# A staging buffer shared out anew at the start of a two-layer transformer kernel

## The chip, the cores and the metric

The kernel runs on one core of a Trainium2 chip. The metric is the device time of one execution in microseconds. The core's engines are TensorE (PE; its weight loads are PEld), VectorE (DVE), ScalarE (ACT), GpSimd (POOL) and SyncE (SP). Each takes its instructions strictly in the order in which the program gives them. Every transfer of this kernel is issued by SP, on one queue.

## What is computed

Two layers, each an attention block with a sliding window and an MLP with squared ReLU, over 2048 rows of 640 values. Both layers use the same weights.

```python
def _A_ref(x, wqkv, wo):           # B, S, D = 1, 2048, 640; H = 32; Dh = 20; W = 256
    q, k, v = ...                  # x @ wqkv, split into 32 heads of 20
    scores = einsum("bhqd,bhkd->bhqk", q, k) * (Dh ** -0.5)
    mask = (i - j >= 0) & (i - j < W)
    p = softmax(where(mask, scores, -1e9))
    return einsum("bhqk,bhkd->bhqd", p, v) ... @ wo
def _B_ref(x, w1, b1, w2, b2):     # F = 1536
    h = x @ w1 + b1
    r = where(h > 0, h, 0)
    return (r * r) @ w2 + b2
x = x + _A_ref(_layernorm(x), wqkv, wo)
x = x + _B_ref(_layernorm(x), w1, b1, w2, b2)   # and both once more
```

## The kernel before

**Units.** The rows are cut into 8 groups of 256; with two layers this gives 16 units, `u = 0..15`. A unit runs through `stage_qk` (queries, then keys), `stage_v`, the attention over 8 quads of 4 heads (`max_quad`: scores and row maxima; `max_out`: the maxima are transposed and written as rows `mT` into the query tile; `exp_quad`: scores again, transposed, and exponentials; `pv_quad`: products with the values), `load_o` and `stage_o` (the attention's result is divided by its sums and multiplied with `wo`), `stage_y` (layernorm, transposed) and `stage_f` (the MLP). The attention of unit u runs beside the queries, keys and values of unit u + 1 and the MLP of unit u - 1.

**Precision.** Each operand of a dense product is split into a high and a low fp16 part, and `mm3` makes three matmuls of it. So whatever leaves a PSUM bank for a later product leaves twice: ACT writes the high part, DVE the low part.

**Banks.** Dense products accumulate in two PSUM banks (tag `mm`), which `mm_tile` hands out in turn. A new product needs a bank whose last content has been evicted.

**Queries and keys.** In `stage_qk` the evictions (line 411 on ACT, 414 on DVE) write a tile `qd`, of which there is one (`bufs=1`). When a unit's queries are complete in it, `leave` sends them to DRAM with two transfers (lines 445 and 447), and the keys of the same unit can be evicted into the tile only when these have left. Unit 0 is an exception: its keys go to the first 1280 columns of the staging buffer `hraw` (`stg`, 3072 fp32 columns).

**Staging buffer.** The second MLP weights, 12 blocks of 640 columns, land in `hraw` and are split there into fp16 parts (`convert`: line 194 on ACT for the high part, then either line 196 on DVE or lines 198 on ACT and 199 on POOL). `load_w2` uses four places for the first four blocks and two places (`c % 2`) for the rest, because unit 0's divided rows `od` (in `load_o`, written by line 760 on ACT and 763 on DVE) take the other half. `load_o(0)` waits for blocks 2 and 3 to be split. The MLP's hidden tile `hh` takes the place of `hraw` afterwards, so its first write waits for all of `w2`.

**Order.** The order on each engine is set when the kernel is built: `Job`, `post`, `pump` and `need` keep a clock for each engine from costs written in the code and emit an instruction when its planned start comes up; dense products are generators that are advanced between attention steps (`flow` for unit 0, `together` for the others). A change of a dependency or a place therefore moves instructions on all engines nearby.

**The end.** For the last unit, `together` leaves part of the dense work of unit 14 unissued. `load_o(15, True)` follows, `upto(dense, 10e3)` issues 10 us (by the planner's costs) of that work while the load runs, then `stage_o(15)`, then the remainder, then the last MLP.

Of the kernel before, what the change touches and what calls it, by code (L numbers as in the profile page):

```python
# [11 lines left out]
F16 = mybir.dt.float16  # L12
# [4 lines left out]
P = 128  # L17
S = 2048
D = 640
# [4 lines left out]
T = 256  # L24
NG = S // T
NU = NL * NG
KC = D // P
# [17 lines left out]
def kernel(ctx: ExitStack, tc: tile.TileContext, x, wqkv, wo, w1, b1, w2, b2, out):  # L45
# [4 lines left out]
    sb = ctx.enter_context(tc.tile_pool(name="sb", bufs=1))  # L50
# [78 lines left out]
    def dma(fn, size, *deps, n=1, cost=450.0, prio=1, **kw):  # L129

        return post("S", n * cost, fn, *deps, prio=prio, size=size, **kw)
# [29 lines left out]
    banks2 = []  # L161
# [25 lines left out]
    w1raw = w1_s.rearrange("p a k n -> p (a k n)").bitcast(F32)  # L187
    w2raw = w2_s.rearrange("p a k n -> p (a k n)").bitcast(F32)
    hraw = sb.tile([P, 2 * FC * T // 2], F32, name="stg", tag="hh", bufs=1)
    gate, gate0 = [Job("S", 0.0, None, [], 0.0, 0) for i in range(2)]  # L190

    def convert(st, hi, low, n, load, *deps, prio=2, dve=True):

# [46 lines left out]
    def load_w2():  # L240
        for c in range(FC):
            first = [w1j[f] for f in (c // 4 * 2, c // 4 * 2 + 1, 6 + c // 4 * 2, 7 + c // 4 * 2)]
            slot = c if c < 4 else c % 2
            st = hraw[:, D * slot:D * (slot + 1)]
            load = dma(lambda st=st, c=c: nc.sync.dma_start(st, w2[c * P:(c + 1) * P, :]), P * D * 4,
                       *([w2j[c - 4 if c < 6 else c - 2]] if c > 3 else [gate]), prio=2, idle=True,
                       land=WLAND)
            w2j[c] = convert(st, w2_s[:, 0, c], w2_s[:, 1, c], D, load, *first, dve=c % 3 == 2)

# [135 lines left out]
    def stage_qk(u, which=(0, 1)):  # L385
        need(*pre.pop(u, ()))
        yT = yTs[u]
        qds = {}

        order = [(j, c0) for j in which for c0 in range(0, KC, 2)]  # L390
        if u == 0:
            order.sort(key=lambda t: t[1])
        for j, c0 in order:
            if j not in qds:
                if j == 0:
                    qts[u] = sb.tile([P, NP, T], F16, name="qt", tag="qt", bufs=2)
                if j and u == 0:
                    qd = hraw[:, :KC * T].bitcast(F16).rearrange("p (c a n) -> p c a n", a=2, n=T)
                elif j and u > 2:
                    qd = beside(u)[:, 1].rearrange("p (c a n) -> p c a n", a=2, n=T)  # L400
                else:
                    qd = sb.tile([P, KC, 2, T], F16, name="qd", tag="qd", bufs=1)
                qds[j] = qd
            qd = qds[j]
            dst = kts[u % 3] if j else qts[u]
            n = min(2, KC - c0)
            acc, jobs = mm_tile([P, 2, T], "acc")
            s = QS / (YS * WS)

            def high(qd=qd, acc=acc, c0=c0, n=n):  # L410
                nc.scalar.activation(qd[:, c0:c0 + n, 0, :], acc[:, :n, :], AF.Copy, scale=s)

            def low(qd=qd, acc=acc, c0=c0, n=n):
                nc.vector.scalar_tensor_tensor(qd[:, c0:c0 + n, 1, :], acc[:, :n, :], s, qd[:, c0:c0 + n, 0, :],  # L414
                                               op0=ALU.mult, op1=ALU.subtract)

            def evict(wait, n=n, c0=c0, high=high, low=low, jobs=jobs, j=j, dst=dst, qd=qd):
                lo_ = post("D", 70 + 267 * n, low, post("A", 60 + 212 * n, high, wait=wait, prio=0), prio=0)
                jobs.append(lo_)
                if u == 0:  # L420
                    leave(u, j, dst, qd, lo_, c0, n)
                elif c0 + n == KC:
                    leave(u, j, dst, qd, lo_, 0, KC)

            for c in range(n):
                lo = j * D + (c0 + c) * P
                need(wqj[lo // P])
                yield from mm3(acc[:, c, :], lambda a, k: wq_s[:, a, k, lo:lo + P],
                               lambda b, k: yT[:, b, k, :], KC, 109, evict if c == n - 1 else None)
# [5 lines left out]
    def leave(u, j, dst, qd, ready, c0, n):  # L435

        if c0 == 0:
            rows_of[u, j] = tc.dram_tile([D, 3, T], F16, name=f"qk{u}_{j}")
        dr = rows_of[u, j]
        drv = dr.rearrange("(c p) t n -> p c t n", p=P)  # L440

        p0, p1 = c0 * P // (2 * DH), (c0 + n) * P // (2 * DH)

        def write():
            nc.sync.dma_start(drv[:, c0:c0 + n, j:j + 2, :].rearrange("p c t n -> p c (t n)"),
                              qd[:, c0:c0 + n].rearrange("p c a n -> p c (a n)"))
            nc.sync.dma_start(drv[:, c0:c0 + n, 2 - 2 * j, :], qd[:, c0:c0 + n, 0, :])

        def spread():
            for e in range(2):  # L450
                nc.sync.dma_start(dst[64 * e:64 * e + 3 * DH, p0:p1, :],
                                  dr.rearrange("(p e d) t n -> e (d t) p n", e=2, d=DH)[e][:, p0:p1])

        wrote = dma(write, n * P * 3 * T * 2, ready, n=2, prio=0)

        def load(*deps):
            job = dma(spread, int((p1 - p0) * 2 * DH * 3 * T * 2 * (1.7 if u > 2 else 1.1)), wrote, *deps, n=2, prio=0)
            for p in range(p0, p1, 2):
                trips[u, j, p // 2] = job
            if u == 0 and j == 1 and p1 == NP:  # L460
                job.gates.append(gate)
            if u == 0 and j == 1 and p0 == 0:
                job.gates.append(gate0)

        if u == 2 and 2 not in rowset:
            held.append((j, load))
        else:
            load(*(rowset.get(u, ()) if j else ()))
# [231 lines left out]

    ols = {}

    def load_o(u, late=False, free_=()):

        l, g = divmod(u, NG)
        if late:
            val = sb.tile([P, KC, T], F32, name="ov", tag="qt", bufs=2)
            od = sb.tile([P, KC, 2, T], F16, name="od", tag="yT", bufs=1)
        elif u == 0:
            val = krow[2][:, :KC * T].rearrange("p (c n) -> p c n", n=T)  # L710
            od = hraw[:, 2 * D:4 * D].bitcast(F16).rearrange("p (c a n) -> p c a n", a=2, n=T)
        else:
            raw = sb.tile([P, 2, KC, T], F32, name="od", tag="hh", bufs=1)
            val = raw[:, 0]
            od = raw[:, 1].rearrange("p c n -> p (c n)").bitcast(F16).rearrange("p (c a n) -> p c a n", a=2, n=T)
# [4 lines left out]
            nc.sync.dma_start(rs, ods[u][DH:].to_broadcast([4, H, T]))  # L720
            nc.sync.dma_start(val, ods[u][:DH].rearrange("(c d) h n -> (d h) c n", d=4))

        loaded = dma(load, P * (KC + 1) * T * 4, *wrote, *free_, n=2, prio=0)
        if u == NU - 1:
            both = sb.tile([P, 2, D], F32, name="x1", tag="qt", bufs=2)
            x1 = [both[:, i] for i in range(2)]
# [177 lines left out]
    late = []  # L904
# [20 lines left out]
            yield c  # L925

    def upto(dense, cost):
        while cost > 0:
            c = next(dense, None)
            if c is None:  # L930
                break
            step(c)
            cost -= c
# [87 lines left out]
    for n in range(NQ):  # L1021
        todo += [("s", n)] + ([("r", n + LEAD - GQ)] if n % GQ == 1 else []) + [("m", n + LEAD), ("v", n)]
    flow(todo, rest)
    load_o(0, False, (w2j[2], w2j[3]))
    left_over = 3 * (QKC + VC + LNC) - used[0]
    rate[0] = 320.0
    for u in range(1, NU):
# [52 lines left out]
```

## Time and profile before

| | |
|---|---|
| median of 3 runs | 1647.06 us (1645.21 to 1647.41) |
| the profiled execution | 1641.93 us, of which its span is 1640.2 us |
| mean granted TensorE clock | 0.987 |
| PE busy | 1575.6 us, 96% of the span |
| DVE, ACT, POOL busy | 1030.1, 748.4, 636.6 us |
| PE busy in the stretches 41 to 82, 123 to 164 us | 28.37 and 29.58 of 41 us |
| granted clock there | 0.83 and 0.81 |

The span is what the profile covers; 1.73 us of the profiled execution lie outside it. The median of the other runs stands 5.13 us above the profiled execution. Busy shares are of the span; the granted clock is the share of full speed that TensorE had.

### The profile page before, as it was taken

The page shows a single profiled execution, that of the slowest core. Times are in us where ns is not written, and L with a number is a line of the kernel's source. Part 1 is how long each engine was busy: PE and PEld are TensorE (multiplying, and loading weights), DVE is VectorE, ACT ScalarE, POOL GpSimd, SP SyncE. Part 2 cuts the span into 40 slices and gives each one's busy share as a digit, 9 for nine tenths or more (in the row PEclk, how much of TensorE's full clock was granted, in tenths as well). Part 3 has the DMA queues.
Part 4 walks back from the last instruction along what each step waited for, and adds up shares of the span by engine and source line. Part 5 has one row for each costly group of instructions (what it writes and reads, how often), then busy time and mean ns, then how long its engine had stood idle before and what let it go on. Part 6 is the DMA issues. An engine that isn't in the chain of part 4 may idle for free.

```text
span 1640.2 us, 52819 instructions
## 1 busy us (share of the span) xinstructions
PE 1575.6 (96%) x21670; PEld 1172.6 (71%) x21670; DVE 1030.1 (63%) x3231; ACT 748.4 (46%) x1616; POOL 636.6 (39%) x1309
## 2 busy tenths in 40 slices
PE   7697899999999999999999999999999999999989
PEld 5564677777777777777777777777777777776667
DVE  7567657675665766566565756657665666757341
ACT  4465534535444454544434354444545444453512
POOL 1343533535344353434414343443534344354412
PEclk9898999999999999999999999999999999999999
DMA  8465214343342434345253434425343452431020
GB/s 255 123 183 157 62 63 109 65 118 86 102 102 65 124 75 112 80 108 114 51 137 74 124 85 103 102 69 119 73 112 81 106 117 51 110 71 54 27 65 17
DMA packets 231517, 157.95 MB, mean 96 GB/s; under 512 B 79468, under 2 KB 215020, under 8 KB 231276
## 3 DMA queue, kind: packets, MB, share of 16 engines
q1 hardware_dynamic: 231276, 154.59, 38.4%
q8 instruction: 170, 2.79, 0.7%
q14 instruction: 71, 0.58, 0.1%
HBM read 84.68 MB, written 52.95 MB: 84 GB/s over the span
## 4 chain that ended last, share of the span: by engine, by line
PE 83%; DVE 6%; ACT 4%; DMA 4%; POOL 2%; issue 1%; SPq 1%; DVEq 0%; ACTq 0%; POOLq 0%
PE acc L256 63%; PE pv L674 10%; PE bb L542 5%; PE bb L613 5%; DVE bb L555 3%; ACT pt L625 2%; DMA qk<-qd 1%; DMA xt<-in_B_b_dram 1%; PE tr L567 1%; POOL x L805 1%; DVE mx L555 1%; POOL pt L644 0%; ACT r L843 0%; DMA w_s<-in_B_w_dram 0%; DMA ov<-o 0%
## 5 line engine op out<-in xcount | busy, mean ns | idle before, releaser
L555 DVE CUSTOM_DVE_ANT_0 bb<-bb,maskb 128x384 f32<-128x384 f32 (+2 forms) x1024 | 510.5, 567 | 114.9 <-PE bb L542 106.4
L625 ACT ACTIVATE pt<-bb 128x512 f32<-128x512 f32 (+1 forms) x736 | 376.5, 601 | 233.9 <-PE bb L613 220.5
L640 POOL TENSOR_SCALAR_AFFINE_SELECT pt<-pt 128x256 f32<-128x256 f32 x448 | 194.8, 439 | 529.7 <-ACT pt L625 507.9
L256 PE MATMUL acc<-y,w_s 128*128 128x256 f16 x2880 | 330.8, 273 | 4.8 <-DVE y L304 1.5
L256 PE MATMUL acc<-w_s,hh 128*128 128x320 f16 x2304 | 326.2, 299 | 0.0
L256 PEld LDWEIGHTS <-w_s 128*128 128x128 f16 x2880 | 277.9, 98 | 57.3 <-issue 23.5
L256 PE MATMUL acc<-yT,wq_s 128*128 128x256 f16 x2400 | 281.0, 275 | 14.0 <-DVE qd L414 11.9
L256 PEld LDWEIGHTS <-hh 128*128 128x128 f16 x2304 | 221.7, 98 | 96.8 <-issue 12.5
L256 PEld LDWEIGHTS <-wq_s 128*128 128x128 f16 x2400 | 232.9, 99 | 57.5 <-issue 26.5
L644 POOL TENSOR_SCALAR_AFFINE_SELECT pt<-pt 128x256 f32<-128x256 f32 x512 | 217.3, 446 | 65.7 <-ACT pt L625 64.6
L853 DVE TENSOR_TENSOR hh<-r,hh 128x256 f16<-128x256 f32 x192 | 91.9, 500 | 205.9 <-ACT hh L850 199.3
L674 PE MATMUL pv<-pt,vt 128*32 128x128 f32 (+1 forms) x3840 | 189.6, 332 | 2.0 <-POOL pt L644 1.4
L847 POOL TENSOR_TENSOR r<-r 128x256 f32<-128x256 f32 x192 | 113.5, 612 | 181.2 <-ACT r L843 179.9
L686 ACT COPY ot<-pv 128x256 f32<-128x256 f32 x128 | 47.6, 372 | 277.4 <-PE pv L674 277.4
L555 DVE DVE_READ_ACCUMULATOR2_ANT mx<- 128x1 f32 x1024 | 145.4, 142 | 0.1
L256 PE MATMUL acc<-wq_s,yT 128*128 128x320 f16 x960 | 142.1, 301 | 0.1
L674 PEld LDWEIGHTS pv<-pt,vt 128*32 128x32 f32 x3840 | 104.4, 110 | 45.6 <-POOL pt L644 4.9
L256 PE MATMUL acc<-wo_s,od 128*128 128x320 f16 x900 | 130.5, 299 | 3.9 <-DVE x L785 1.7
L843 ACT ACTIVATE r<-acc,b1s 128x256 f32<-128x256 f32 x192 | 80.6, 471 | 98.0 <-PE acc L256 97.2
L256 PEld LDWEIGHTS <-yT 128*128 128x128 f16 x960 | 93.1, 99 | 40.4 <-issue 6.5
L256 PEld LDWEIGHTS <-od 128*128 128x128 f16 x900 | 85.5, 98 | 44.7 <-issue 8.3
L613 PE MATMUL bb<-qt,kt 62*64 62x128 f16 (+3 forms) x3840 | 100.3, 235 | 9.1 <-DVE mx L555 8.4
(84 smaller groups left out, 1169.5 us busy)
## 6 DMA issues: line engine op xcount, KB each, us to landing
qt<-qk SPq DMA_DIRECT2D x30, 480.0 KB
kt<-qk SPq DMA_DIRECT2D x30, 480.0 KB
qk<-qd SPq DMA_DIRECT2D x17, 640.0 KB
o<-ot SPq DMA_DIRECT2D x256, 42.0 KB
od<-o SPq DMA_DIRECT2D x13, 640.0 KB
qk<-yl SPq DMA_DIRECT2D x13, 640.0 KB
qk<-qd SPq DMA_DIRECT2D x17, 320.0 KB
xt<-in_A_x_dram SPq DMA_DIRECT2D x16, 320.0 KB
```

What stands on the lines that cost most here:

```text
L256: nc.tensor.matmul(acc, lhs(a, c), rhs(b, c), start=(k == 0), stop=(k == 3 * nk - 1))
L542: nc.tensor.matmul(to, qt[r, p, i * P + 64 * h:i * P + 64 * h + 64], kt[r, p, a:b], start=True, stop=True, tile_position=(64 * e, 64 * h))
L555: nc.vector.tensor_tensor_reduce(out=v, in0=v, in1=mask, scale=1.0, scalar=-3.0e38, op0=ALU.add, op1=ALU.max, accum_out=accum)))
L613: nc.tensor.matmul(bb[e][64 * h:64 * h + 64, k, o:o + w], kt[r, p, ko + 64 * h:ko + 64 * h + 64], qt[r, p, q:q + w], start=True, stop=True ...
L625: nc.scalar.activation(box["pt"][:, :o], bb[e][:, k, :o], AF.Exp, scale=SCALE / (QS * QS))
L640: nc.gpsimd.affine_select(out=m, in_=m, pattern=[[0, 2], [-1, P]], compare_op=ALU.is_gt, fill=0.0, base=0, channel_multiplier=1)
L644: nc.gpsimd.affine_select(out=m, in_=m, pattern=[[0, 2], [1, P]], compare_op=ALU.is_ge, fill=0.0, base=0, channel_multiplier=-1)
L674: nc.tensor.matmul(pv[32 * jj:32 * (jj + 1), q0 * P:(q0 + qn) * P], vf[:, c:c + 32], pj[:, j, :], start=(k == 0), stop=(k == len(steps) - ...
L686: nc.scalar.copy(ot[:, qd % 2], pv)
L843: nc.scalar.activation(box["r"], acc[:, f, :], AF.Relu, bias=b1s[:, f0 + f:f0 + f + 1], scale=1.0 / (YS * WS))
L847: nc.gpsimd.tensor_tensor(box["r"], box["r"], box["r"], op=ALU.mult)
L853: nc.vector.tensor_sub(hh[:, 1, f, :], box["r"], hh[:, 0, f, :])
```

## The change

Four edits. Unit 1's keys are evicted into the second 1280 columns of `hraw` instead of the one `qd` tile. Unit 0's divided rows `od` get a tile of their own, under the tag `qd`, and no longer wait for weight blocks. All twelve blocks of the second MLP weights go through four places, and those of the second half wait until unit 1's keys have left. `upto` goes on until each open bank has been given its eviction, so the kept work ends with a whole product.

```diff
-    gate, gate0 = [Job("S", 0.0, None, [], 0.0, 0) for i in range(2)]
+    gate, gate0, gate1 = [Job("S", 0.0, None, [], 0.0, 0) for i in range(3)]
     def load_w2():
-            slot = c if c < 4 else c % 2
+            slot = c % 4
-                       *([w2j[c - 4 if c < 6 else c - 2]] if c > 3 else [gate]), prio=2, idle=True,
+                       *([w2j[c - 4]] if c > 3 else [gate, gate1][:1 + c // 2]), prio=2, idle=True,
     def stage_qk(u, which=(0, 1)):
-                if j and u == 0:
-                    qd = hraw[:, :KC * T].bitcast(F16).rearrange("p (c a n) -> p c a n", a=2, n=T)
+                if j and u < 2:
+                    qd = hraw[:, u * KC * T:][:, :KC * T].bitcast(F16).rearrange("p (c a n) -> p c a n", a=2, n=T)
     def leave(u, j, dst, qd, ready, c0, n):
         wrote = dma(write, n * P * 3 * T * 2, ready, n=2, prio=0)
+        if u == 1 and j:
+            wrote.gates.append(gate1)
-    def load_o(u, late=False, free_=()):
+    def load_o(u, late=False):
         elif u == 0:
             val = krow[2][:, :KC * T].rearrange("p (c n) -> p c n", n=T)
-            od = hraw[:, 2 * D:4 * D].bitcast(F16).rearrange("p (c a n) -> p c a n", a=2, n=T)
+            od = sb.tile([P, KC, 2, T], F16, name="od", tag="qd", bufs=1)
-        loaded = dma(load, P * (KC + 1) * T * 4, *wrote, *free_, n=2, prio=0)
+        loaded = dma(load, P * (KC + 1) * T * 4, *wrote, n=2, prio=0)
     def upto(dense, cost):
-        while cost > 0:
+        while cost > 0 or not all(banks2):
-    load_o(0, False, (w2j[2], w2j[3]))
+    load_o(0)
```

Two lines are added above the attention, so line numbers from 457 on are two higher in the changed kernel (its line 582 is line 580 of before). The text below uses the numbers of before.

The order of PE's instructions is the same in both up to the end of the last unit. Three places where the order or the target of other engines moves:

First, ACT around the eviction of unit 1's first keys. `qd` is the one tile, `stg` the staging buffer, `pt` the exponentials, `ot` the attention's result. Before:

```order
L686 COPY ot<-pv 128x256
L198 ACTIVATE w_s<-w_s 128x640
L194 ACTIVATE wo_s<-w_s 128x640
L411 ACTIVATE qd<-acc 128x2x256
L625 ACTIVATE pt<-bb 128x512 x2
```

and now:

```order
L688 COPY ot<-pv 128x256
L198 ACTIVATE w_s<-w_s 128x640
L194 ACTIVATE wo_s<-w_s 128x640
L411 ACTIVATE stg<-acc 128x2x256
L627 ACTIVATE pt<-bb 128x512 x2
```

The order is the same; the eviction's target is another buffer.

Second, SP after the last part of unit 0's attention result `o` has been sent. `rs` and `kt_79` receive the sums and the undivided rows of `load_o(0)`, `qk_1` takes unit 2's keys, and `stg` the blocks of the second MLP weights. Before:

```order
L691 DMA o_808<-ot 21x2x256 x4
L245 DMA stg<-in_B_w_dram 128x640
L445 DMA qk_1_1829<-qd 128x5x512
L447 DMA qk_1_1829<-qd 128x5x256
L245 DMA stg<-in_B_w_dram 128x640 x2
L720 DMA rs<-o_808 128x1x256
L721 DMA kt_79<-o_808 128x5x256
L580 DMA qt<-mT 1x8x128 x4
L451 DMA qt<-qk_0_1494 60x16x256 x2
```

and now:

```order
L693 DMA o_807<-ot 21x2x256 x4
L245 DMA stg<-in_B_w_dram 128x640
L722 DMA rs<-o_807 128x1x256
L723 DMA kt_79<-o_807 128x5x256
L445 DMA qk_1_1829<-qd 128x5x512
L447 DMA qk_1_1829<-qd 128x5x256
L451 DMA qt<-qk_0_1493 60x16x256 x2
L737 DMA x_1779<-in_A_x_dram 128x640
L737 DMA x_1780<-in_A_x_dram 128x640
L245 DMA stg<-in_B_w_dram 128x640
L582 DMA qt<-mT 1x8x128 x4
```

The two loads of `load_o(0)` have moved ahead of unit 2's keys and of two weight blocks; the row copies `mT` have moved behind a weight block.

Third, DVE at the same stage: `rs` is inverted, `kt_79` multiplied with it, `od` (before: `stg`) takes the low part, `yT` is the transposed layernorm for unit 3. Before:

```order
L196 SCALAR_TENSOR_TENSOR w_s<-stg,w_s 128x640
L572 TENSOR_SCALAR mT<-tr 16x128
L573 SCALAR_TENSOR_TENSOR mT<-tr,mT 16x128
L304 TENSOR_TENSOR yT<-tr,yT 128x3x128
L304 TENSOR_TENSOR yT<-tr,yT 128x2x128
L304 TENSOR_TENSOR yT<-tr,yT 128x3x128
L304 TENSOR_TENSOR yT<-tr,yT 128x2x128
L753 RECIPROCAL rs<-rs 128x64 x2
L756 TENSOR_TENSOR kt_79<-kt_79,rs 128x5x64 x2
L196 SCALAR_TENSOR_TENSOR w_s<-stg,w_s 128x640
L763 TENSOR_TENSOR stg<-kt_79,stg 128x5x64 x2
```

and now:

```order
L196 SCALAR_TENSOR_TENSOR w_s<-stg,w_s 128x640
L755 RECIPROCAL rs<-rs 128x64 x2
L574 TENSOR_SCALAR mT<-tr 16x128
L575 SCALAR_TENSOR_TENSOR mT<-tr,mT 16x128
L758 TENSOR_TENSOR kt_79<-kt_79,rs 128x5x64 x2
L755 RECIPROCAL rs<-rs 128x64
L765 TENSOR_TENSOR od<-kt_79,od 128x5x64 x2
L758 TENSOR_TENSOR kt_79<-kt_79,rs 128x5x64
L304 TENSOR_TENSOR yT<-tr,yT 128x3x128
L304 TENSOR_TENSOR yT<-tr,yT 128x2x128
L755 RECIPROCAL rs<-rs 128x64
```

The division and the first half of `od` stand ahead of the layernorm's transposes now, and the weight block has moved behind. The fourth low part of `od` and three fills of `kt_79`, which before stood after the row maxima of the next quad, stand ahead of them.

At the end, PE issues 108 of the 144 matmuls of unit 14's second MLP product ahead of `stage_o(15)`, where it issued 76 before; a product is 36 matmuls.

## The prediction

> **What bounds the kernel now.** I read the page first, then PE's waits, then the stretches in which those waits lie, engine by engine. In the page, PE is busy 96% of the span, and the chain that ended last is PE for 83% of it.
>
> ```profile
> PE 1575.6 (96%) x21670; PEld 1172.6 (71%) x21670; DVE 1030.1 (63%) x3231; ACT 748.4 (46%) x1616; POOL 636.6 (39%) x1309
> PE 83%; DVE 6%; ACT 4%; DMA 4%; POOL 2%; issue 1%; SPq 1%; DVEq 0%; ACTq 0%; POOLq 0%
> ```
>
> So only 64.6 us are to be had from filling PE's gaps, and whatever time PE spends at a lower clock. PE's waits (total us, times, longest) name where:
>
> ```profile
> PE acc L256 <- DVE qd L414: 11.9, 1, 11.9
> PE bb L613 <- DVE mx L555: 8.4, 11, 3.0
> ...
> PE acc L256 <- ACT stg L760: 4.1, 1, 4.1
> PE tr L300 <- DVE xt L286: 3.1, 1, 3.1
> PE acc L256 <- DVE stg L763: 2.9, 2, 2.1
> ```
>
> The first is a wait for keys to be evicted, the third and fifth are for `od`. The change touches these, and four short ones at the end. It leaves the second and fourth alone: PE's order there is the same, and the work around them hardly moves.
>
> **Unit 1's keys.** Rows in the timeline give start, duration, engine, operation, and in brackets the idle time before.
>
> ```profile
> 45.83 5.63 PE L256 MATMUL acc<-yT,wq_s 128*128 128x256 f16 x50
> 69.62 2.29 PE L256 MATMUL acc<-yT,wq_s 128*128 128x256 f16 x10 [11.89 <-DVE qd L414]
> 77.03 0.52 PE L613 MATMUL bb<-qt,kt 62*64 62x256 f16 x16
> 57.81 0.74 ACT L194 ACTIVATE wo_s<-w_s 128x640 f16<-128x640 f32 x1 [1.78 <-DMA w_s<-in_A_wo_dram]
> 68.24 0.60 ACT L411 ACTIVATE qd<-acc 128x512 f16<-128x512 f32 x1 [9.70 <-DMA qk<-qd]
> 57.83 3.27 SPq L447 DMA_DIRECT2D qk<-qd  x1
> 69.78 2.83 SPq L580 DMA_DIRECT2D qt<-mT  x4
> 57.83 10.31 DMA qk<-qd
> 66.00:68.00 2.00, 0.00 (x0) 0.00 (x0) 0.00 (x0) 0.00 (x0) 0.00 (x0) 0.50 0.21 68
> ```
>
> PE stops at 57.73 (69.62 - 11.89) because its next product needs the bank of the first keys. ACT cannot evict them before unit 1's queries have left `qd`: their write (the row of the chain, 10.31) ends at 68.14. With a place of their own the keys wait for ACT alone, which is held until 58.50 by a weight conversion (57.81 + 0.74, overlapping the next). From ACT's start to PE's restart the trace shows 69.62 - 68.24 = 1.38, so PE would restart at 59.88. The wait falls from 11.89 to 2.15: 9.7 us.
>
> What is late next: PE's `exp_quad` (line 613) follows 77.03 - 69.62 = 7.41 after the restart, at 67.29, and needs the row maxima `mT` in `qt`. SP's four copies of them started 0.16 after PE's restart (69.78), so they are due at 60.0; but SP is issuing the queries' second write until 61.10, so they go out from 61.1 to 63.9 (2.83) behind a write that lands only at 68.14. In the trace the same copies are used 7.25 after their issue without a wait, with nothing ahead of them. So the added wait lies between 0 (they pass) and about 3 (they land after 68.14 by the length of their own issue). The last row (PE to POOL busy, granted clock 0.50, DMA share 0.21) shows a fifth of the DMA engines' time still busy just before 68; I take the middle, 1.5. [...] No row before shows small copies behind a large write with a waiting reader.
>
> Net for this edit 8.2 us. Ends: 5.0 (the rows cost 3 and PE's clock falls once more, 1.7, half of the 3.5 below) and 10.9 (no wait for rows, and the restart at full clock: 10 matmuls took 2.29, where 50 of them took 5.63 at 45.83, so 1.2). Later loads and conversions keep their order behind this place and move up with it; DMA was one fifth used at the end of these ten microseconds, so what covers them stays.
>
> **Unit 0's divided rows.**
>
> ```profile
> 143.39 0.83 PE L300 MATMUL tr<-ident,xt 128*128 128x128 f32 x5 [0.53 <-DVE yT L304]
> 148.34 0.71 PE L256 MATMUL acc<-wo_s,stg 128*128 128x320 f16 x2 [4.12 <-ACT stg L760]
> 149.88 2.85 PE L256 MATMUL acc<-wo_s,stg 128*128 128x320 f16 x10 [0.83 <-DVE stg L763]
> 152.65 1.49 PE L542 MATMUL bb<-kt,qt 60*64 60x128 f16 x36
> 154.08 1.98 PE L674 MATMUL pv<-pt,vt 128*32 128x256 f32 x32
> ...
> 161.15 1.08 PE L256 MATMUL acc<-wo_s,stg 128*128 128x320 f16 x6 [2.10 <-DVE stg L763]
> 162.16 1.50 PE L613 MATMUL bb<-qt,kt 62*64 62x256 f16 x32
> 163.59 4.00 PE L256 MATMUL acc<-wo_s,stg 128*128 128x320 f16 x22
> 261.55 2.21 PE L256 MATMUL acc<-wo_s,od 128*128 128x320 f16 x15
> 126.32 0.36 SPq L245 DMA_DIRECT2D stg<-in_B_w_dram  x1
> 135.53 2.20 SPq L245 DMA_DIRECT2D stg<-in_B_w_dram  x2
> 137.83 0.59 SPq L720 DMA_DIRECT2D rs<-o  x1
> 140.92 2.75 SPq L580 DMA_DIRECT2D qt<-mT  x4
> 145.29 0.95 DVE L753 RECIPROCAL rs<-rs 128x64 f32<-128x64 f32 x2
> 147.45 0.83 ACT L760 CAST stg<-kt 128x320 f16<-128x320 f32 x2
> 134.09 1.42 POOL L199 TENSOR_TENSOR w_s<-stg,w_s 128x640 f16<-128x640 f32 x1 [0.23 <-ACT stg L198]
> ```
>
> (In the times of before; all of it moves up by the 8.2.) The load of `rs` leaves at 137.83, behind two weight blocks that SP held until 135.53 for POOL's conversions. Now it stands ahead of both and of unit 2's keys, behind the block at 126.32; with some 3 us for the last part of `o` to land, that is 8 us earlier. DVE can divide before the layernorm's transposes instead of behind them. `od` wants the one `qd` tile: unit 2's keys go out at about 130, and even with the 10.31 of unit 1's queries they have left it at 140.6, before DVE's first product behind `mT` (140.92). So that adds nothing. But the transposes are now late: two of DVE's divisions (0.95) and two of ACT's casts (0.83) stand ahead of them, so the x5 transposes start near 145.1 instead of 143.39. The first product follows 1.6 later, at 146.75, instead of 148.34, without the second wait (0.83) and the third (2.10).
>
> The clock adds to it. The 22 matmuls at 163.59 take 182 ns each, against 147 for the 15 at 261.55 (4.00/22 and 2.21/15): after 2.10 us of waiting PE runs slow for some 3.5 us. [...]
>
> Stepping through PE's rows from 146.75: 12 matmuls still slow (3.5), scores and values 1.2 and 1.6 (1.49 and 1.98 slow), 26 matmuls 3.8, which is 156.9; 0.3 more for DVE's maxima, which the third wait hid so far; then scores 0.9 (1.50 slow) and 22 x 0.147 = 3.2. The product ends at 161.3 instead of 167.6 (163.59 + 4.00). I take 6.2 us. Ends: 8.5 (the transposes not late, no slow restart) and 3.0 (only the last two waits, 2.93, go).
>
> **Four places for the weights.** Unit 0's hidden tile must wait for all of `w2`, so ACT's casts come late:
>
> ```profile
> 191.13 1.02 ACT L850 CAST hh<-r 128x256 f16<-128x256 f32 x3 [3.46 <-DVE w_s L196]
> 197.05 0.21 PE L542 MATMUL bb<-kt,qt 60*64 60x128 f16 x1 [1.20 <-ACT pt L625]
> ```
>
> With four places the blocks are in sooner, and the casts stand between other work. PE loses only 1.20 here, from exponentials queued behind the casts; I take 0.8, between 0 and 1.5.
>
> **The end.**
>
> ```profile
> 1563.12 10.49 PE L256 MATMUL acc<-w_s,hh 128*128 128x320 f16 x76
> 1574.10 2.34 PE L256 MATMUL acc<-wo_s,od 128*128 128x320 f16 x15 [0.48 <-DVE kt L880]
> ...
> 1582.58 2.20 PE L256 MATMUL acc<-wo_s,od 128*128 128x320 f16 x15 [0.58 <-DVE x L785]
> ...
> 1593.85 0.49 PE L300 MATMUL bb<-ident,xt 128*128 128x128 f32 x3
> 1577.89 0.49 DVE L763 TENSOR_TENSOR od<-ov,od 128x320 f16<-128x320 f32 x1 [0.53 <-ACT od L760]
> 1587.19 0.61 DVE L286 TENSOR_SCALAR xt<-x,bmv 128x640 f32<-128x640 f32 x1 [0.66 <-POOL bmv L284]
> ```
>
> 76 matmuls are two products and four matmuls of a third, which keep one bank open, so the four `wo` products share the other and each waits for an eviction (0.48, and 0.58 three times). With 108 both banks are free. From 1563.12, 204 matmuls of 10.49/76 = 0.138 end at 1591.3 instead of 1593.85: 2.4 us (2.2, the waits alone, to 2.6). The 32 matmuls moved ahead had hidden the last layernorm: it ends (1587.19 + 0.61) 3.0 after the last `wo` product (1582.58 + 2.20), so at 1589.3 behind products that now end at 1586.3. That is still 2.0 ahead of PE. The last part of `od` (1577.89 + 0.49) is needed at 1582.1.
>
> **Sum.** 8.2 + 6.2 + 0.8 + 2.4 = 17.6 us off the profiled execution of 1641.93: 1624.3. That execution ran 5.13 below the median of 1647.06; set against the median the sum gives 1629.5, and I predict 1630. With all terms at their ends the gain is 10.2 to 23.5, so 1624 to 1637.
>
> **Rivals.** *The row copies become the wait* (14%). Unit 1's wait turns into one for `qt` and the first term stays at its low end or less: 14.4 in all, 1633. For it speaks the write still draining at 66 to 68, against it that the copies are only 2 KB each.
>
> *The divided rows are no sooner* (15%). DVE and ACT are given the division ahead of the transposes, and PE waits there instead; the second term falls to about 1: 12.4, 1635. For it speaks that the order now puts this work ahead of what PE waits for at 143.39. With the first rival 1638.
>
> *The gain is given back* (5%). All of the front's work is moved up against loads that do not move, and PE waits at a later weight load for as long as it saved: only the end's 2.4 stays, 1645. Against it speaks that PE's list of waits holds none for a weight load, and that DMA was mostly idle in the wait that goes (0.21 in the row above).
>
> *SP is blocked* (3%, slower). The copies of `mT` (140.92) stand behind a weight block that waits for POOL's conversion of the first block, which ended at 135.51 (134.09 + 1.42). Their reader is the scores at 162.16, near 157 then; less 2.75 for the copies, a conversion ending after 154 costs PE one for one, 18.7 later than it does. The kernel is slower from another 20.9 on (17.6 and the 3.3 below): with a conversion 45 us late it would be 1656. POOL's wait ahead of it was 0.23.
>
> **Chances.** My forecast holds 63%. What a measurement can tell from no change is 0.2%, 3.3 us. Faster takes the forecast and the first two rivals, 0.92; the third rival is within 0.2%, 0.05; slower 0.03. The range runs from 1622, past the best sum, to 1639, past the first two rivals together.
>
> **What would show it.** Right: PE's wait for line 414 near 60 is about 2 us instead of 11.89, no wait of PE for lines 760 or 763 near 135, four `wo` products without gaps at the end. Wrong: a wait of a few us at line 613 near 67, or one for line 304 before the first `wo` product.

## The result, and the profile after

The changed kernel takes 1629.20 us (median of 5 runs, 1623.36 to 1631.56), the kernel before 1645.21 beside it (1641.41 to 1647.41): a ratio of 0.9899, with a 95% interval of 0.9873 to 0.9925. The ratio is estimated from all runs and isn't the quotient of the two medians. By the medians the gain is 16.0 us, by the interval 12.3 to 20.9. The profiled execution took 1627.51, its span 1625.8, at a granted clock of 0.993. A second series, with a second profile, gave 1628.71 (1622.82 to 1631.08) against 1644.63: 0.9896 [0.9879, 0.9914], span 1623.2. Both profiles are used below, since they differ in an instructive way.

The page after, its engines and its chain:

```profile
PE 1573.4 (97%) x21670; PEld 1172.1 (72%) x21670; DVE 1030.1 (63%) x3231; ACT 749.9 (46%) x1616; POOL 641.0 (39%) x1309
PE 87%; DVE 5%; ACT 3%; DMA 2%; issue 1%; POOL 1%; SPq 0%; DVEq 0%; POOLq 0%; ACTq 0%
```

PE does the same work in 2.2 us less busy time; the other 12.2 us between the spans are idle time that went. PE's waits after:

```profile
PE bb L615 <- DVE mx L557: 10.3, 15, 3.0
...
PE tr L300 <- DVE xt L286: 4.4, 1, 4.4
PE bb L615 <- DMA qt<-mT: 3.8, 1, 3.8
...
PE acc L256 <- DVE stg L414: 1.1, 1, 1.1
```

The wait of 11.89 us for the keys' eviction is 1.1, and the three for `od` near 148 to 161 are gone. New is a wait of 3.8 us for the row copies `mT`. Two waits that the prediction left alone have grown: the layernorm's (line 300) from 3.13 to 4.40, and those for the row maxima `mx` from 8.4 to 10.3 in total (9.0 in the second profile).

To see where the time lies, the program is cut into six stretches at seven places. Each place is the start of one matmul that all kernels share: the transposition of the row maxima (`tr<-ident,mx`), and at the last place the last recorded group on PE. Us between these places, from PE's timeline; the starts in the row of before are 57.45, 84.05, 140.30, 180.72, 204.19, 1534.97 and 1617.25:

| kernel | keys | up to the rows | divided rows | places | middle | end |
|---|---|---|---|---|---|---|
| before | 26.60 | 56.25 | 40.42 | 23.47 | 1330.78 | 82.28 |
| after, first profile | 19.96 | 56.74 | 35.83 | 23.08 | 1329.66 | 79.28 |
| after, second profile | 18.60 | 56.00 | 32.78 | 23.08 | 1331.18 | 79.29 |
| keys alone | 20.17 | 55.96 | 40.29 | 23.48 | 1331.96 | 83.87 |
| rows and places alone | 26.15 | 57.34 | 32.81 | 23.08 | 1331.10 | 81.94 |
| rows alone | 27.01 | 57.35 | 35.47 | 28.31 | 1330.40 | 81.85 |
| end alone | 26.39 | 57.33 | 40.03 | 23.48 | 1330.83 | 80.97 |
| after, with two places | 20.29 | 59.28 | 35.68 | 28.40 | 1329.17 | 79.30 |

In the first profile the keys' stretch gives 6.6, the divided rows' 4.6, the places' 0.4 and the end 3.0; in the second 8.0, 7.6, 0.4 and 3.0. Ahead of the first place, where nothing is changed, the profiles of this table differ by up to 2.6 us, and the two profiles of the changed kernel differ by 3.05 in one stretch: a difference of 2 us between two profiles is no evidence by itself. In the rows keys alone and end alone the last stretch holds some 1.6 us of lower clock that the others don't have: the same 179 matmuls take 21.31 and 21.37 there and 19.70 in every other row (see the last section).

### The profile page after: what moved, and what is told of

It is laid out like the page before. It is cut to its first block, busy times and chain, and to the rows that moved or that the text cites. A ratio compares the mean times of both kernels' runs of the same rounds, so it can differ in the third digit from the quotient of the medians.

```text
span 1625.8 us, 52818 instructions
## 1 busy us (share of the span) xinstructions
PE 1573.4 (97%) x21670; PEld 1172.1 (72%) x21670; DVE 1030.1 (63%) x3231; ACT 749.9 (46%) x1616; POOL 641.0 (39%) x1309
## 4 chain that ended last, share of the span: by engine, by line
PE 87%; DVE 5%; ACT 3%; DMA 2%; issue 1%; POOL 1%; SPq 0%; DVEq 0%; POOLq 0%; ACTq 0%
PE acc L256 66%; PE pv L676 10%; PE bb L615 5%; PE bb L544 5%; DVE bb L557 2%; ACT pt L627 1%; PE tr L569 1%; DMA w_s<-in_A_wo_dram 1%; DVE mx L557 0%; DMA qk<-qd 0%; DMA xt<-in_B_b_dram 0%; DMA w_s<-in_A_wqkv_dram 0%; POOL pt L646 0%; DVE mT L574 0%; DMA qt<-mT 0%
## 5 line engine op out<-in xcount | busy, mean ns | idle before, releaser
L256 PE MATMUL acc<-wo_s,od 128*128 128x320 f16 x960 | 140.3, 301 | 2.4 <-DVE od L765 1.7
L256 PEld LDWEIGHTS <-od 128*128 128x128 f16 x960 | 91.9, 98 | 46.2 <-issue 7.4
L615 PE MATMUL bb<-qt,kt 62*64 62x128 f16 (+3 forms) x3840 | 100.8, 235 | 14.6 <-DVE mx L557 10.3
```

Source lines behind the costliest of these rows:

```text
L256: nc.tensor.matmul(acc, lhs(a, c), rhs(b, c), start=(k == 0), stop=(k == 3 * nk - 1))
L615: nc.tensor.matmul(bb[e][64 * h:64 * h + 64, k, o:o + w], kt[r, p, ko + 64 * h:ko + 64 * h + 64], qt[r, p, q:q + w], start=True, stop=True ...
```

## The experiments

**One part of the change at a time.** Kernel before, with the keys' edits only:

```diff
...
-                if j and u == 0:
-                    qd = hraw[:, :KC * T]...
+                if j and u < 2:
+                    qd = hraw[:, u * KC * T:][:, :KC * T]...
-                       *([w2j[c - 4 if c < 6 else c - 2]] if c > 3 else [gate])
+                       *([w2j[c - 4 if c < 6 else c - 2]] if c > 3 else [gate, gate1][:1 + c // 2])
+        if u == 1 and j:
+            wrote.gates.append(gate1)
```

> The kernel before with one part of the change alone: unit 1's keys leave from the staging buffer, and the second-weight blocks that would overwrite that buffer wait for it. Divided rows, the places for the second weights and the kept work at the end stand as before. Theory (the term is what the trace of the changed kernel shows between the transposes at the unit's end, 6.6 us, and it depends on nothing else in the change): 6 to 7 us faster than before, with TensorE's wait for the row copies near 69 us at about 3.8 us and the wait for the bank near 60 us at about 1. Rival (the sum of the prediction): 8.2 us faster, with a row-copy wait near 1.5. Rival (the gain leaned on the other parts and is given back at the next wait, for the divided rows): under 2 us faster, with the wait at the output projection near 142 longer by the missing amount.

Measured: 1638.04 against 1644.63, 0.9950 [0.9934, 0.9966], so 6.6 us faster by the medians. The interval, 5.6 to 10.9 us, holds the theory's 6 to 7 and the first rival's 8.2, so the time doesn't decide between them. In the trace the keys' stretch is 6.4 shorter, in PE's timeline with these rows:

```profile
59.17 2.29 PE L256 MATMUL acc<-yT,wq_s 128*128 128x256 f16 x10 [1.68 <-DVE stg L414]
68.48 0.88 PE L615 MATMUL bb<-qt,kt 62*64 62x256 f16 x16 [1.91 <-DMA qt<-mT]
70.28 3.03 PE L256 MATMUL acc<-wq_s,yT 128*128 128x320 f16 x12
```

The wait for the copies is 1.91, not the expected 3.8, because the products ahead of it ran slower (10 of them 2.29, in the changed kernel 1.25); the scores (68.48) start 11.26 after the first place (57.22), in the changed kernel 11.05 after it. So the end of this wait is fixed by the copies, however early PE arrives. The gain is not given back later: the next stretches are those of before.

The kernel before with the two edits that belong to `od`, rows and places:

```diff
-            slot = c if c < 4 else c % 2
+            slot = c % 4
-                       *([w2j[c - 4 if c < 6 else c - 2]] if c > 3 else [gate])
+                       *([w2j[c - 4]] if c > 3 else [gate])
-            od = hraw[:, 2 * D:4 * D]...
+            od = sb.tile([P, KC, 2, T], F16, name="od", tag="qd", bufs=1)
-    load_o(0, False, (w2j[2], w2j[3]))
+    load_o(0)
```

> The kernel before with two parts alone: the first divided rows have a buffer of their own and the second weights have four places; the keys and the kept work at the end stand as before. Theory (the rows' term is 6.6 us at the output projection, of which about 2 are given back at the layernorm behind it, plus 0.2 for the places): 4 to 5.5 us faster than before, with TensorE's wait for the layernorm's rows at about 4.4 us, before 3.1. Rival (the give-back belongs to the keys, which bring the block forward against loads that did not move): 6 to 7 us faster and a layernorm wait of about 3.1.

Measured: 1638.77, 0.9954 [0.9939, 0.9969], 5.9 us faster by the medians. The interval, 5.1 to 10.0 us, doesn't decide between the theory and the rival; the layernorm's wait does. It is 4.40 without the keys' edits, so the give-back belongs to the rows and places, as expected. In the profile the rows' stretch is 7.6 shorter.

The kernel before with the edit in `upto` only:

```diff
-        while cost > 0:
+        while cost > 0 or not all(banks2):
```

> The kernel before with one part alone: the last unit's kept work ends with a product, so that 108 matmuls stand ahead of the last output projection where there were 76. Theory (the gap ahead of that projection closes): 2.2 to 3.0 us faster than before, all of it behind 1560 us. Rival (part of the 3.0 us between the profiles is chance of one run): 2.0 or less.

Measured: 1642.52 (10 runs), 0.9982 [0.9973, 0.9992], 2.1 us faster by the medians, 1.3 to 4.4 by the interval, so the time doesn't decide between the theory and the rival. The traces do: from the start of the 108 matmuls (76 before) to the first transposition of the last layernorm (line 300) PE takes 27.71 here and in the changed kernel, and 30.28 to 30.73 in the four kernels without this edit. So 2.6 to 3.0 us are gained, and not by chance of one run. By the medians the three parts add up to 6.6 + 5.9 + 2.1 = 14.6, and the whole gives 16.0: within the intervals they add up.

**Rows and places taken apart.** The changed kernel with two places again:

```diff
-            slot = c % 4
+            slot = c if c < 4 else c % 2
-                       *([w2j[c - 4]] if c > 3 else ...
+                       *([w2j[c - 4 if c < 6 else c - 2]] if c > 3 else ...
```

> The changed kernel with two places for the MLP's second weights instead of four; everything else as changed. Theory (four places take away only the waits of 1.2 us and less near 187 us): 0 to 1 us slower than the changed kernel, so about 15 us faster than before, with the layernorm wait at about 4.4 us still. Rival (four places let later blocks be split earlier, beside the layernorm, and so cause its longer wait): the layernorm wait falls to about 3.1 us, and the kernel is as fast as the changed one or up to 1 us faster.

Measured: 1635.21, 0.9929 [0.9912, 0.9945]; 0.9929 against 0.9899 is 4.9 us slower than the changed kernel, whose runs in both series (1622.82 to 1631.56) all lie below the runs here (1631.64 to 1635.38). Its trace has a wait of 3.98 for ACT's ReLU in the stretch called places, and a layernorm's wait of 3.84. Both expectations missed. So the remaining part was tried in the kernel before by itself, the `od` and `load_o(0)` lines of the diff above without the `slot` lines:

> The kernel before with the own place for the first divided rows alone; the second weights keep two places from the fourth block on, and keys and end stand as before. The run with two places in the changed kernel lost 4.9 us between the second and the third transposes of the MLP (173.8 to 202.2, against 170.8 to 193.9), to a wait of 4.0 us for ScalarE's ReLU, which stood behind the blocks' conversions. Theory (the two parts are one: without four places the gain of the rows turns into that wait): about 7 us gained to the output projection, 4 to 5 of them lost again near 190, so 2 to 3 us faster than before, against 5.9 for the two parts together. Rival (that wait comes from the keys, which move the rest forward as well): 5 to 6 us faster, and no wait above 1.5 near 190.

Measured: 1642.66 (10 runs) against 1643.98, 0.9995 [0.9983, 1.0008]: no gain, less even than the theory left, though by its mechanism. By the profile the rows' stretch is 5.0 shorter, and the next one 4.8 longer. PE, then ACT in that stretch of rows alone:

```profile
190.24 2.90 PE L256 MATMUL acc<-y,w_s 128*128 128x256 f16 x25
197.11 3.36 PE L256 MATMUL acc<-y,w_s 128*128 128x256 f16 x15 [3.97 <-ACT r L843]
190.40 3.04 ACT L625 ACTIVATE pt<-bb 128x512 f32<-128x512 f32 x6 [3.80 <-PE bb L613]
193.28 0.78 ACT L194 ACTIVATE w_s<-stg 128x640 f16<-128x640 f32 x1
195.01 1.32 ACT L850 CAST hh<-r 128x256 f16<-128x256 f32 x4 [0.95 <-DVE w_s L196]
196.24 1.56 ACT L843 ACTIVATE r<-acc,b1s 128x256 f32<-128x256 f32 x4
```

PE waits 3.97 for a bank that ACT's ReLU (line 843) must empty. The ReLU stands behind the hidden tile's casts (line 850), and the first of these waits for the last weight block, because `hh` takes the place of `hraw`. How many blocks are late is read from the groups by line, for line 194, one of which belongs to each block. The three rows are: before in the rows' stretch (140.30 to 180.72), rows alone in its rows' stretch, and rows alone in the stretch behind:

```profile
L194 ACT ACTIVATE w_s<-stg 128x640 f16<-128x640 f32 x7 | 5.0, 739 | 0.0
L194 ACT ACTIVATE w_s<-stg 128x640 f16<-128x640 f32 x5 | 3.7, 743 | 0.0
L194 ACT ACTIVATE w_s<-stg 128x640 f16<-128x640 f32 x3 | 2.3, 775 | 0.0
```

Before, PE's waits for `od` gave two more blocks time to pass through the two places, and one was left for the next stretch. Without those waits three are left. With four places all eight are through before it (the changed kernel, 134.95 to 170.78):

```profile
L194 ACT ACTIVATE w_s<-stg 128x640 f16<-128x640 f32 x8 | 5.9, 738 | 0.0
```

So the own tile for `od` brings nothing without the four places. Four places without the own tile were not run; in the kernel before, `od` lies in two of the four.

**What holds the row copies.** In the changed kernel, SP's queue and behind it PE's reader:

```profile
51.27 0.79 SPq L232 DMA_DIRECT2D w_s<-in_B_w_dram  x1
53.16 4.58 SPq L445 DMA_DIRECT2D qk<-qd  x1
57.78 3.49 SPq L447 DMA_DIRECT2D qk<-qd  x1
61.37 4.71 SPq L582 DMA_DIRECT2D qt<-mT  x4
69.30 0.88 PE L615 MATMUL bb<-qt,kt 62*64 62x256 f16 x16 [3.77 <-DMA qt<-mT]
70.72 3.41 PE L256 MATMUL acc<-wq_s,yT 128*128 128x320 f16 x12
```

The copies are issued when the queries' write has been, and used 7.93 after the first issue. Two edits were tried. In the first, the load of line 232 (640 KB) goes out behind the copies:

```diff
...
-            load = dma(lambda st=st, f0=f0: nc.sync.dma_start(...), P * KC * 2 * P * 4, gate,
+            def fetch(st=st, f0=f0): nc.sync.dma_start(...)
+            load = dma((lambda fetch=fetch: held_w1.append(fetch)) if f0 == 0 else fetch, ..., gate,
...
+            if (u, G) == (0, 1):
+                held_w1.pop()()
```

> The changed kernel with one transfer moved: the first load of the MLP's first weights (640 KB) is issued on SP right behind the four row copies near 66 us instead of ahead of unit 1's queries near 51. Question: what makes TensorE wait 3.8 us near 69 for the row copies, which SP issues as the last of some 14 us of issues without a pause (1.0 + 4.6 + 3.5 + 4.7 us). Theory (the issues of the queries' write are slow because the load ahead of them still fills the DMA engines): the two queries' issues fall from 4.6 and 3.5 us to under 2 each, the row copies come 4 to 6 us sooner, the wait near 69 is under 0.5, and the kernel is 2 to 4 us faster than the changed one, so 18 to 20 faster than before. Rival A (SP's issues of these four transfers cost what they cost, for the number of pieces they are cut into): only the load's own 0.8 to 1.2 us leaves the row, the wait falls to 2.5 to 3, and the kernel gains about 1. Rival B (the later load is missed where it is used): a new wait of some us for the first block of it, and no gain.

Measured: 1625.83 (1624.51 to 1626.44), 0.9886 [0.9864, 0.9908]. SP and PE of this kernel, and a stretch of 1 us with its DMA share:

```profile
53.76 0.38 SPq L448 DMA_DIRECT2D qk<-qd  x1
54.19 3.60 SPq L450 DMA_DIRECT2D qk<-qd  x1
60.08 3.65 SPq L585 DMA_DIRECT2D qt<-mT  x4
63.79 0.43 SPq L235 DMA_DIRECT2D w_s<-in_B_w_dram  x1
67.36 0.92 PE L620 MATMUL bb<-qt,kt 62*64 62x256 f16 x16 [1.57 <-DMA qt<-mT]
62.00:63.00 1.00, 1.00 (x18) 0.73 (x11) 1.00 (x9) 0.53 (x2) 0.69 (x1) 1.00 0.27 104
```

The queries' first issue falls from 4.58 to 0.38: it was slow because the load had gone ahead of it. The second does not change (3.60), so half of the theory fell, and with it the wait under 0.5. SP is now free at 57.79, before the rows are written, so SP no longer holds the copies. The scores start 8.52 after the first place (58.84), 2.5 sooner than in the changed kernel. A wait of 1.57 stays: the copies take 7.28 from their first issue to use, nearly as long as in the changed kernel (7.93).

The trace's records of single DMA packets show what they wait for. Each copy is eight packets of 256 bytes, 32 in all. In the changed kernel 16 of them run from 64.59 to 66.77, in the pace of SP's issues. The other 16 run only from 67.41 to 68.55, in four groups, each directly behind the end of a run of 512-byte packets of the queries' write. With the load moved the two halves run from 62.40 to 64.43 and from 65.70 to 66.60. In the kernel before, where the write had landed, all 32 run from 71.10 to 73.33. So half of each copy waits until the queries' write is through, even when SP has long issued it. In all seven profiles in which SP issues the copies while the write is under way, their last packet ends 0.08 after the write's last. With the load moved the write ends sooner, and the scores with it: 7.67 after the first place instead of 10.22.

The write in turn runs beside the three loads of `wo` issued just ahead of it (line 224): their 384 packets of 2560 bytes run until 63.87, about 40 per us of 0.102 us each, which is the work of some four engines (an estimate from these two numbers; the last row above, a stretch from 62 to 63 with 0.27 of the 16 DMA engines' time busy, agrees). A quarter of the write's 512-byte packets, 160 of 640, runs only after that. That moving these loads would help was not tried.

In the second, the four copies are issued by ACT:

```diff
-                    nc.sync.dma_start(qt[r:r + 1, ...
+                    (nc.scalar if (u, G) == (0, 1) else nc.sync).dma_start(qt[r:r + 1, ...
```

> The changed kernel with one edit: the four row copies near 61 to 66 us are issued from ScalarE's queue instead of SP's; nothing else is moved. Theory (they are late because they stand behind 8 us of issues on SP, and not because of the DMA engines): issued within 1 us of the rows being written, near 60, they land before TensorE comes to them at 65.5; the wait near 69 goes, ScalarE loses up to 4 us to issues (where SP paid 4.7) with no more than 1 of it seen by TensorE; 2 to 3.5 us faster than the changed kernel. Rival (the DMA engines are full with the load and the queries' write until about 67): the copies land no sooner than near 68, the wait stays at 3 us or more, and the time is the changed kernel's within 1, or slower for the issues on ScalarE.

Measured: 1630.50, 0.9914 [0.9886, 0.9941], like the changed kernel. The price of an issue moved with it, onto an engine that PE needs (ACT, PE):

```profile
61.30 3.60 ACTq L582 DMA_DIRECT2D qt<-mT  x4
64.95 1.15 ACT L627 ACTIVATE pt<-bb 128x512 f32<-128x512 f32 x3 [4.11 <-DMA qt<-mT]
65.88 1.13 PE L544 MATMUL bb<-kt,qt 60*64 60x128 f16 x20 [3.07 <-ACT pt L627]
```

The wait for the copies is gone, since PE now stands 3.07 for ACT instead. I had put that at 1 us. By the packets the copies land at 68.33, which is 8.98 after the first place (59.35), where the changed kernel has 10.30. That is 1.3 sooner, and still far from the theory's 65.5: SP's issues are not all that holds them. Here they end 0.90 ahead of the write's last packet and not behind it. PE comes to them only at 73.53.

**The layernorm's wait.** The changed kernel, with the low parts of blocks 8 to 11 held back:

```diff
...
-            w2j[c] = convert(..., dve=c % 3 == 2)
+            w2j[c] = convert(..., dve=c % 3 == 2, then=gate3 if c > 7 else None)
...
+        if u == 0:
+            js[0].gates.append(gate3)
```

> The changed kernel with the low parts of blocks 8 to 11 of the MLP's second weights held back until unit 0's first add of the second bias, so that they leave VectorE and GpSimd during the layernorm near 158 to 161 us. Theory (the layernorm's wait grew from 3.13 to 4.40 us because its last steps stand beside these conversions: 1.68 us against 0.61 for the 640-wide scale, 1.06 against 0.56 for the one-number step): the wait falls to 3.1 or less and the scale to about 0.6, 1 to 1.5 us faster than the changed kernel, less what the later conversions cost behind it (up to 0.5). Rival (the wait grew because the divided rows came sooner than the residual they are added to): the wait stays near 4.4 and the time the same.

Measured: 1627.91, 0.9902 [0.9876, 0.9928]. The last steps of the layernorm, POOL then DVE then PE, in the changed kernel and, below the dots, with the blocks held:

```profile
158.17 1.06 POOL L284 TENSOR_TENSOR bmv<-bmv,neghalf 128x1 f32<-128x1 f32 x1 [1.02 <-DVE bmv L278]
159.21 1.39 POOL L199 TENSOR_TENSOR w_s<-stg,w_s 128x640 f16<-128x640 f32 x1
159.27 1.68 DVE L286 TENSOR_SCALAR xt<-x,bmv 128x640 f32<-128x640 f32 x1 [0.45 <-POOL bmv L284]
161.10 0.87 PE L300 MATMUL tr<-ident,xt 128*128 128x128 f32 x3 [4.40 <-DVE xt L286]
...
157.67 0.56 POOL L284 TENSOR_TENSOR bmv<-bmv,neghalf 128x1 f32<-128x1 f32 x1 [1.03 <-DVE bmv L278]
158.27 0.61 DVE L286 TENSOR_SCALAR xt<-x,bmv 128x640 f32<-128x640 f32 x1 [0.68 <-POOL bmv L284]
159.03 0.87 PE L300 MATMUL tr<-ident,xt 128*128 128x128 f32 x3 [2.83 <-DVE xt L286]
```

DVE's scale takes 0.61 with the blocks held and 1.68 when POOL's conversion has started 0.06 ahead of it: 1.07 longer, most of the 1.33 that the conversion still runs. Why the conversion beside it makes it longer is shown by no run. The wait falls by 1.57, as expected. But the blocks are missed later: the stretch called places takes 24.06 instead of 23.08, so 1.0 is given back, and the run's time shows no gain.

**Both together**, beside the second series of the changed kernel:

> The changed kernel itself, on the chip and beside the runs of before that the next run shares, so that the two can be compared. Expected: 0.988 to 0.992 of before. The profile is there for the clock: if the half clock near 139 to 146 (behind waits of 0.17, 1.08 and 0.81 us) is chance, it may be missing this time, and the output projection's first twelve products take 1.8 us instead of 3.4; the wait for the layernorm stays at 4.4 either way.

> The changed kernel with both later edits: the first load of the first weights behind the four row copies, and the low parts of blocks 8 to 11 held until unit 0's first add of the second bias. Theory (the two act at different places, near 67 and near 159 us): 2.0 us from the copies and 1.3 from the layernorm (1.6 less its wait, 0.7 of half clock behind it, 1.0 lost again near 180), so 3.3 us below the changed kernel run beside it, 0.9855 to 0.989 of before. Rival (what is gained at the layernorm is lost again where the later blocks are used, as the time of the run with that edit alone says): 2 us below it or less.

Measured: 1628.71 (in whose profile the twelve products take 1.79 us, as expected if the half clock is chance) and, with both edits, 1626.28 (1624.33 to 1627.67), 0.9885 [0.9869, 0.9901]; the changed kernel is 0.9896 [0.9879, 0.9914]. With both it is 2.4 below the changed kernel, between the theory's 3.3 and the rival's 2 or less. The intervals overlap, so neither this nor the moved load alone (1625.83) is shown to beat the changed kernel; that the slowest of their runs, 1627.67, lies below its median points that way.

## Why the prediction came out, and where it did not

The forecast was 1630, and 1629.2 was measured. That they are so near is partly luck. The forecast was set against a median of 1647.06, which is 1645.21 with two more runs, and the 17.6 forecast as the gain came out as 16.0; the two errors cancel. The sum, 17.6 off 1641.93, is 1624.3; the two profiled executions took 1627.51 and 1624.90. The total is right; of its terms only some are.

**Unit 1's keys, 8.2 forecast.** The restart was sized right, and for the reason given. The scores were due at 68.79 (67.29 and a wait of 1.5), which is 11.34 after the first place; they start 11.05 and 11.36 after it in the two profiles, and 19.58 before (77.03). The prediction left open between two bounds whether they pass the queries' write. They land with its end: by the packets the second half of each copy runs directly behind the write's, and ends 0.08 after them. The 1.5 itself was a middle between two bounds and no result.

The split between the two waits was not right. The bank's wait is 1.13 (2.15 forecast), and the copies' 3.77 (1.5, end 3), since the products between them ran faster than in the trace of before (10 of them 1.25, before 2.29) and PE came sooner to copies that land when they land. SP's slow issues (4.71 for the copies, 2.83 forecast) have a share: without the write, the first half alone (66.77, and 0.75 from the last packet to the scores) would still have cost 2.0, an estimate from these rows. The row copies do become a wait, as the first rival says, though without its price. What failed is the clock behind the wait, which the sum left out and only the low end held (1.7): the 12 products at 70.72 take 3.41, at a granted clock of 0.50 (70.7 to 74.0), and 1.79 in the second profile, so that 6.6 remain at the end of the stretch. In the second profile the clock falls ahead of the copies' wait (granted clock 0.50 from 63 to 65), which covers it, and 8.0 remain:

```profile
61.54 1.61 PE L256 MATMUL acc<-yT,wq_s 128*128 128x256 f16 x10 [1.98 <-DVE stg L414]
70.64 0.88 PE L615 MATMUL bb<-qt,kt 62*64 62x256 f16 x16 [1.71 <-DMA qt<-mT]
72.00 1.79 PE L256 MATMUL acc<-wq_s,yT 128*128 128x320 f16 x12
```

**Unit 0's divided rows, 6.2 forecast.** 4.6 and 7.6 in the two profiles, from the same instructions. PE's rows at the same place, first and, below the dots, second profile:

```profile
137.98 0.44 PE L300 MATMUL tr<-ident,xt 128*128 128x128 f32 x2 [1.08 <-ACT vt L482]
139.22 1.33 PE L300 MATMUL tr<-ident,xt 128*128 128x128 f32 x5 [0.81 <-DVE yT L304]
141.28 3.36 PE L256 MATMUL acc<-wo_s,od 128*128 128x320 f16 x12 [0.73 <-DVE yT L304]
...
136.91 0.44 PE L300 MATMUL tr<-ident,xt 128*128 128x128 f32 x2 [1.08 <-ACT vt L482]
138.16 0.77 PE L300 MATMUL tr<-ident,xt 128*128 128x128 f32 x5 [0.81 <-DVE yT L304]
139.96 1.79 PE L256 MATMUL acc<-wo_s,od 128*128 128x320 f16 x12 [1.03 <-DVE yT L304]
```

The waits for `od` went, as forecast, and no wait on lines 760 or 763 stands there. The first product was forecast 6.45 after the place (146.75 less 140.30) and starts 6.33 and 6.08 after it; of the second rival, only waits of 0.81 and 0.73 (1.03 in the second profile) for line 304 came true. The step "12 matmuls still slow" holds in the first profile and fails in the second, after waits of nearly the same length. At the end of the product, for which the 6.2 was worked out, 6.6 and 8.9 us are gained; behind it 2.0 and 1.3 are given back. What failed there is the line that leaves the layernorm's wait alone: it is longer by 4.40 - 3.13 = 1.3.

**Four places, 0.8 forecast.** As a term by itself this is wrong. It was read off a wait of 1.20 in the trace of before, where PE's waits for `od` covered the conversions; the second term removes just these. In the changed kernel four places are worth 4.9 us by the times, and rows alone nothing. Together the two were forecast at 7.0, and 5.9 was measured by the medians. My line on the third rival, that PE's waits hold none for a weight load, missed this: it would have come as a wait for ACT's ReLU.

**The end, 2.4 forecast.** 3.0 in both profiles. PE's rows after:

```profile
1551.68 14.83 PE L256 MATMUL acc<-w_s,hh 128*128 128x320 f16 x108
1566.35 8.31 PE L256 MATMUL acc<-wo_s,od 128*128 128x320 f16 x60
1574.50 5.05 PE L256 MATMUL acc<-w_s,hh 128*128 128x320 f16 x36
1579.39 0.49 PE L300 MATMUL bb<-ident,xt 128*128 128x128 f32 x3
```

The four `wo` products have no gaps, as forecast. The 204 matmuls take 27.71, or 0.136 each. The 0.138 of the prediction counts in the end of the last matmul, which the next run of matmuls overlaps: the 108 end at 1566.51, and the 60 start at 1566.35, 0.16 sooner. A gap takes this overlap away, so each costs PE some 0.16 besides its wait of 0.5, an estimate from these two rows. Of the 0.63 by which the four groups of before (2.34 + 3 x 2.20 = 8.94) exceed the 60 in one run (8.31), the three gaps between them explain 0.48 in this way.

**The rival on the slower side** (SP blocked by a weight block) did not happen: no wait of PE for `mT` stands near 150 in either profile.

## What to carry to other kernels

A wait that goes takes with it the cover for all that ran during it. Before a small wait elsewhere is priced from the old trace, ask which engine caught up during the large one; two edits that look separate may be worth something only together. And when a buffer's wait is removed, the next limit is the queue behind it. Read what the issuing engine does in those microseconds, and when the large transfers ahead will have landed: a small copy can wait for them (half of the row copies' packets ran only behind the end of the queries' write), and a load issued early can cost it more than the load's own issue (0.79 us here, where the scores came 2.5 sooner with the load moved).

## What the runs showed of the hardware

**Behind the same chain of short waits the clock fell in five profiles of twelve.** In the end's last layernorm, PE waits 0.57, 0.96 and 0.60 us, in every profile. The same 179 matmuls follow. They take 19.70 in seven of the twelve profiles and 21.16 to 21.37 in five; here are the second profile of the changed kernel and the one with the blocks held:

```profile
1580.68 19.70 PE L256 MATMUL acc<-y,w_s 128*128 128x256 f16 x179 [0.60 <-DVE y L304]
1581.84 21.37 PE L256 MATMUL acc<-y,w_s 128*128 128x256 f16 x179 [0.60 <-DVE y L304]
```

The difference, 1.67, is a start at lower clock: 0.50 is granted from 1583 to 1585 in the slow one, and 1.00 throughout in the other. With the 1.4 and 3.05 by which the changed kernel's two profiles differ at the keys and at the divided rows, such places add up to some 6 us, and the changed kernel's own runs span 8.7. In the slow profiles three waits of under 1 us stood ahead of the lower clock, as they did in the others ahead of the full one. What decides between the two is shown by no run.

**What a DMA issue cost its engine depended on what had been issued ahead.** The queries' first write took 4.58 us to issue behind a load of 640 KB and 0.38 without it. The four copies cost SP 4.71 in the changed kernel, 3.65 with the load moved and 2.83 in the kernel before, where the write had landed; ACT paid 3.60 for them.

**The small row copies landed behind the large write that SP had issued ahead of them.** Issued by SP, the last of the 32 packets ends 0.08 us after the write's last in seven profiles of seven; issued by ACT, in one profile, 0.90 before it.
